# Seven products within seven products: second-layer outputs by two levels of Winograd's scheme, with weight blocks kept in DRAM

## The chip, the cores and the metric

The kernel runs on one core of one Trainium2 chip. The metric is the device time of one execution in microseconds (us). Engines are named as in the profile: PE multiplies matrices, DVE, ACT and POOL (VectorE, ScalarE, GpSimd) work elementwise, SP issues most DMAs. A PE result goes to PSUM, of which there are eight banks of 128 x 512 f32.

## The reference

The reference has two parts. The first is an attention in both directions between tokens x (8 batches, 8 heads, 512 tokens, 64 values) and 32 states per head. Its result, 8 x (512 + 32) rows of 512 values, goes through a feed-forward layer of 2048 hidden units:

```
scores = x @ state^T / 8;  a = softmax(scores);  xread = a @ state
scores2 = state @ x^T / 8; a2 = softmax(scores2); sread = a2 @ x
x2 = concat([xread, sread]) as rows (8 * 544) x 512
h = x2 @ w_in            # 512 x 2048
g = h * cos(h)
out = g @ w_out          # 2048 x 512
```

Everything is f32.

## The kernel before, in words

The main loop (L965) runs over 144 tiles. For each batch b there are 16 tiles; tile f is 128 hidden units for all 512 tokens of the batch, held transposed (hidden unit on the partition, token along the row). Sixteen more tiles take the state rows of all batches at once (256 columns). The attention of batch b+1 is done in parts beside the tiles of batch b, by a plan written out by hand (`plan`, L875: which part at which step on which engine). Attention and `w_in` are merged: `products` (L430) multiplies states with `w_in`, giving `sw`, and the first layer is then `sw` times the softmax weights `aT` (K = 256). Order on every engine is the order of the program text (`manual_schedule`, L56).

A tile goes through `hidden` (L463: two matmuls into a PSUM bank `h`), `gate` (L560, ACT: round to an integer), `gate2` (L564, DVE: difference), `gate3` (L567, ACT: sine) and `gate4` (L571, DVE: times h, into the SBUF array `g_all`).

Both layers use seven block products in place of eight (Winograd's form of Strassen's scheme). In the first layer this is done for tiles of batches 2 to 7 whose `phase` is under 3 (`seven`, L474). Two tiles f, f+1 go together: `hidden_a` (L521) and `hidden_b` (L544) make seven products of 256 columns in PSUM, and `sums_a` (L534) and `sums_b` (L551) add them up on DVE in SBUF (ACT copies one half first, L531). The sums of weight blocks (`sw_sums`, L496) are made on POOL, those of `aT` (`halves`, L482) on DVE.

In the second layer, two batches make a `Pair` (L585). The pair's hidden rows are four blocks (its `phase`: batch even or odd, hidden units lower or upper half), `w_out` is four blocks a11 to a22 with sums s1 to s4 kept in SBUF (`blocks`, L949). Differences of hidden blocks, of 128 x 512 each, are taken one tile at a time by `minus` (L579), on POOL or DVE. Each product is eight tiles times two matmuls of 512 columns (`product`, L617), accumulated in two of four PSUM banks `acc`. A tile's output products (`output`, L698) come `LAG` = 3 tiles after its gates, so the first layer and the gates run ahead of the outputs; p7 and p4 of a pair are done among the tiles of the next pair (`more`, L600). `keep_product` and `plus` (L629, L624) take a product to the array `held`; `store` (L646) transposes it on DVE and sends it by four DMAs on SP. The state rows' outputs are made at the end (`state_products`, L762), again by seven products.

Weights come as f32 bit patterns from DRAM and are converted in steps 0 to 16 (`convert_part`, L215, on ACT, DVE and POOL). A few dummy matmuls (`warm`, L837) fill PE at the start.

The names steps, periods and end are used so: a step is one turn of the main loop; a period is the 32 steps of a pair; the end is steps 128 to 143 (state tiles) and `state_products`.

## Time and profile before

| | us |
|---|---|
| median of 3 runs | 758.56 |
| lowest, highest | 758.52, 759.78 |
| the profiled execution | 759.83 |
| its span, first to last instruction | 758.0 |
| PE busy in the span | 747.9 |
| DVE, ACT, POOL busy | 519.9, 313.2, 256.6 |

A group of the profile gives line, engine, operation and tiles, then the time in which at least one of its instructions ran and the mean of one. Matmuls overlap in a pipeline, so a mean of 599 ns for a matmul pass of 512 columns is not its price; the distance from one to the next is. PEld is the weight load, which runs beside the matmul before. Idle time has behind it what ended it.

### The profile page before, as it was taken

How to read it: one execution, taken by the hardware profiler on the slowest of the kernel's cores; microseconds unless marked ns; L12 is line 12 of the kernel's file. 1: busy time of each engine (PE TensorE's matmuls, PEld its weight loads, DVE VectorE, ACT ScalarE, POOL GpSimd, SP SyncE). 2: the span in 40 equal slices, each digit the busy share in tenths (PEclk: the TensorE clock that was granted, in tenths of full speed). 3: DMA queues.
4: the chain of work that ended last, by engine and by line, in shares of the span. 5: the costliest groups of instructions: out<-in, count | busy, mean ns of one | idle time of the engine just before them, and what ended most of it. 6: DMA issues, size and time to landing. Idle time of an engine off the chain costs nothing.

```text
span 758.0 us, 8557 instructions
## 1 busy us (share of the span) xinstructions
PE 747.9 (99%) x2928; PEld 389.7 (51%) x2928; DVE 519.9 (69%) x883; ACT 313.2 (41%) x522; POOL 256.6 (34%) x265
## 2 busy tenths in 40 slices
PE   8998999999999999999999999999999999999998
PEld 3443443445555554445555554445555554466666
DVE  5778778736886788846886888747877675434630
ACT  3887843533363435333363336432453333212210
POOL 2354278777121212663121113661121126510000
PEclk9999999999999999999999999999999999999999
DMA  8595471060012510160104310350100110101031
GB/s 249 169 277 200 137 105 29 4 108 1 5 23 37 100 23 10 23 117 0 19 11 75 64 29 1 50 90 1 28 1 1 28 29 0 29 0 29 8 48 28
DMA packets 161291, 41.46 MB, mean 55 GB/s; under 512 B 154016, under 2 KB 154528, under 8 KB 161248
## 3 DMA queue, kind: packets, MB, share of 16 engines
q1 hardware_dynamic: 160160, 40.39, 25.3%
q10 hardware_dynamic: 960, 0.39, 0.2%
q8 instruction: 23, 0.38, 0.2%
q14 instruction: 20, 0.16, 0.1%
q0 software_dynamic: 128, 0.13, 0.1%
HBM read 31.98 MB, written 8.91 MB: 54 GB/s over the span
## 4 chain that ended last, share of the span: by engine, by line
PE 92%; DVE 3%; ACT 1%; DMA 1%; POOL 1%; issue 1%; SPq 0%; DVEq 0%; ACTq 0%; POOLq 0%
PE o L619 51%; PE h L466 15%; PE h L509 14%; PE at L314 5%; PE o L772 2%; PE at L404 2%; PE o L314 1%; PE at L772 1%; PE at L387 1%; DMA x_b<-in_x_dram 1%; ACT q L568 0%; DVE i L328 0%; ACT q L562 0%; PE o L840 0%; POOL g_all L581 0%
## 5 line engine op out<-in xcount | busy, mean ns | idle before, releaser
L619 PE MATMUL o<-g_all,w_out 128*128 128x512 f32 x512 | 237.4, 599 | 0.6 <-POOL w_out L237 0.3
L619 PE MATMUL o<-g_all,s 128*128 128x512 f32 x384 | 177.3, 598 | 0.0
L581 POOL TENSOR_TENSOR g_all<-g_all 128x512 f32<-128x512 f32 x89 | 124.7, 1422 | 107.2 <-DVE g_all L575 107.2
L619 PEld LDWEIGHTS o<-g_all,w_out 128*128 128x128 f32 x512 | 93.8, 190 | 108.6 <-issue 102.6
L568 ACT ACTIVATE q<-q,halfpi 128x512 f32<-128x512 f32 (+1 forms) x144 | 100.7, 700 | 91.1 <-DVE q L565 90.9
L619 PEld LDWEIGHTS o<-g_all,s 128*128 128x128 f32 x384 | 70.8, 190 | 88.1 <-issue 84.4
L466 PE MATMUL h<-aT,sw 128*128 128x512 f32 x224 | 106.4, 598 | 2.9 <-DVE g_all L575 2.4
L562 ACT ACTIVATE q<-g_all 128x512 int32<-128x512 f32 x75 | 46.8, 624 | 142.2 <-DVE g_all L555 141.8
L565 DVE TENSOR_TENSOR q<-q,h 128x512 f32<-128x512 int32 (+1 forms) x69 | 42.9, 622 | 81.6 <-ACT q L562 81.5
L562 ACT ACTIVATE q<-h 128x512 int32<-128x512 f32 (+1 forms) x69 | 37.6, 545 | 108.0 <-PE h L466 108.0
L565 DVE TENSOR_TENSOR q<-q,g_all 128x512 f32<-128x512 int32 x75 | 52.9, 705 | 36.0 <-ACT q L562 36.0
L466 PEld LDWEIGHTS h<-aT,sw 128*128 128x128 f32 x224 | 41.9, 190 | 56.6 <-issue 45.7
L504 POOL TENSOR_TENSOR swS<-sw 128x128 f32<-128x128 f32 x35 | 17.6, 502 | 147.6 <-PE h L509 107.3
L575 DVE TENSOR_TENSOR g_all<-g_all,q 128x512 f32<-128x512 f32 x75 | 54.2, 722 | 14.3 <-ACT q L568 14.3
L575 DVE TENSOR_TENSOR g_all<-h,q 128x512 f32<-128x512 f32 (+1 forms) x69 | 42.9, 622 | 22.8 <-ACT q L568 21.9
L504 POOL TENSOR_TENSOR swS<-sw,swS 128x128 f32<-128x128 f32 x35 | 18.3, 523 | 87.1 <-PE h L509 86.7
L509 PEld LDWEIGHTS h<-aT,sw 128*128 128x128 f32 x144 | 27.4, 190 | 34.4 <-issue 28.5
L509 PE MATMUL h<-aS,sw 128*128 128x256 f32 x144 | 43.1, 381 | 0.1
L509 PE MATMUL h<-aT,sw 128*128 128x256 f32 x144 | 42.8, 379 | 0.0
L509 PE MATMUL h<-aS,swS 128*128 128x256 f32 x144 | 42.8, 379 | 0.0
L237 POOL TENSOR_TENSOR w_in<-w_in,s 128x1024 int32<-128x1024 int32 (+1 forms) x10 | 19.3, 1932 | 36.8 <-DVE w_in L232 22.0
L466 PE MATMUL h<-st_all,w_in 128*128 128x256 f32 x128 | 30.2, 379 | 0.0
(109 smaller groups left out, 889.0 us busy)
## 6 DMA issues: line engine op xcount, KB each, us to landing
g_all<-in_moe_w_out_dram SPq DMA_DIRECT2D x8, 1024.0 KB, 5.1
out_dram<-ot SPq DMA_DIRECT2D x128, 64.0 KB, 2.0
g_all<-in_moe_w_in_dram SPq DMA_DIRECT2D x6, 1024.0 KB, 5.3
xT<-in_x_dram SPq DMA_DIRECT2D x96, 64.0 KB, 2.3
x_b<-in_x_dram SPq DMA_DIRECT2D x24, 256.0 KB, 4.6
x_b<-in_x_dram SPq DMA_DIRECT2D x16, 128.0 KB, 4.0
g_all<-in_moe_w_in_dram SPq DMA_DIRECT2D x4, 512.0 KB, 6.0
s<-in_state_dram SPq DMA_DIRECT2D x8, 32.0 KB, 7.3
```

The source lines that it names most:

```text
L237: nc.gpsimd.tensor_tensor(bits, bits, e, op=ALU.add)
L314: nc.tensor.matmul(out=(to or at)[j][Ns * k:Ns * k + Ns, 0:n], lhsT=w[D * j:D * j + D, self.b, Ns * k:Ns * k + Ns], rhs=r(slice(D * j, D * ...
L466: nc.tensor.matmul(out=t.hp, lhsT=t.lhs(i), rhs=t.rhs(i), start=(i == 0), stop=(i == t.kn - 1))
L504: engine.tensor_tensor(o, x1, x2, op=op)
L509: nc.tensor.matmul(out=out, lhsT=w, rhs=r, start=True, stop=True)
L562: nc.scalar.activation(t.q.bitcast(I32), t.hp, func=ACTF.Copy, bias=0.25)
L565: nc.vector.tensor_tensor(t.q, t.q.bitcast(I32), t.hp, op=ALU.subtract)
L568: nc.scalar.activation(t.q, t.q, func=ACTF.Sin, bias=halfpi, scale=-TWO_PI)
L575: nc.vector.tensor_tensor(t.g, t.hp, t.q, op=ALU.mult)
L581: engine.tensor_tensor(out, a, b, op=ALU.subtract)
L619: nc.tensor.matmul(out=acc[bank][ch], lhsT=w[:, i, P * ch:P * ch + P], rhs=g.g, start=(i == 0), stop=(i == NH - 1))
L772: nc.tensor.matmul(out=x, lhsT=b(i), rhs=w[:, i, :], start=(start and i == 0), stop=(i == NH - 1), skip_group_check=True)
```

## The change

The second layer's products are split once more: each of a pair's seven products (eight tiles times 256 output columns) becomes seven products of half the size in every direction. Only p1 and p2 of the first pair stay as they were. In the code:

- `Product` is one of the outer seven; its seven `stage`s are the inner products, each of four matmuls of 256 columns. They share two PSUM banks, b and c: a stage writes half a bank, ACT copies a half into the other bank as a seed (k = 0) or to SBUF (k = 1), later stages add to what is there, and DVE adds two halves (k = 2, 4). `out` then takes a bank to `held` as before, and POOL adds totals.
- `sums` makes the four inner sums of hidden blocks on POOL (128 x 4 x 256 each). The outer differences (`outer_sum`) now go by four tiles at once (128 x 2048), five per pair on DVE and three on POOL.
- `inner_weights` makes the inner sums of the seven outer weight blocks on POOL in steps 9 to 26, and SP writes the 56 blocks of 256 KB to DRAM. `fetch_block` reads one per stage into a ring of four; at the end `load_end_weights` reads those for the state rows. `weight_sum` makes the outer weight sums on DVE.
- `plan_products` sets the stages at a fixed pace: 49 stages over a period of 32 steps, for the last pair 28 stages over 15 steps. There is no `LAG` any more. The products of a pair lie in the period after its own, apart from p1, p2 and p5.
- In the first layer, `seven_part` and `seven_sum` replace `hidden_a`, `hidden_b`, `sums_a` and `sums_b`: the seven products are put together within two banks, in four parts over two steps, two steps ahead of the gates; ACT makes two copies, DVE two additions, and the gates read PSUM. The pool of banks `h` grows from two to four, `acc` shrinks from four to two.
- Loads of x are put in a list and sent by `load_now`, eight per step at first and then four.

The diff, cut to its core:

```diff
-    hps = ctx.enter_context(tc.tile_pool(name="hps", bufs=2, space=PSUM))
+    hps = ctx.enter_context(tc.tile_pool(name="hps", bufs=4, space=PSUM))
...
+    QT, NQUAD = 4, 12
+    g_all = consts.tile([P, (NQUAD + 1) * QT, S], F32)
+    TEMPS = 4
+    quads_free = list(range(TEMPS))
+    def quad(n):
+        return g_all[:, QT * n:QT * n + QT]
+    def matrix(n):
+        return quad(n).rearrange("p t (u d) -> p (t u) d", d=HD)
+    a11, a12, a21, a22 = [matrix(n) for n in range(5, 9)]
+    w_out = ((a11, a12), (a21, a22))
+    NB = 4
+    ring = [g_all[:, QT * NQUAD + i].rearrange("p (i d) -> p i d", d=P)
+            for i in range(NB)]
+    spare = ctx.enter_context(tc.tile_pool(name="spare", bufs=1,
+                                           space=bass.MemoryType.DRAM))
+    blocks_kept = spare.tile([7, 8, P, QT * P], F32)
...
+    aS_all = consts.tile([P, 2, 4, HS], F32)
+    p5_all = consts.tile([P, 2, HS], F32)
+    swS_all = consts.tile([P, 2, 3, P], F32)
...
+    def load_now(n):
+        for _ in range(min(n, len(loads_due))):
+            dst, src = loads_due.pop(0)
+            nc.sync.dma_start(out=dst, in_=src)
...
-    acc = [[ops.tile([P, S], F32, name=f"o{m}{ch}") for ch in range(2)]
-           for m in range(2)]
+    acc = [ops.tile([P, S], F32, name=f"o{ch}") for ch in range(2)]
+    def side_banks():
+        return [hps.tile([P, S], F32, name="h") for _ in range(2)]
...
+    def seven_part(t, k):
+        (b11, b12, b21, b22), swS = weights_of(t)
+        aT, aS = aT_of[t.b], aS_all[:, t.b % 2]
+        if k == 0:
+            t.h1, t.h2 = side_banks()
+        h1, h2 = t.h1, t.h2
+        for out_, w, r, start in (
+                ((h2[:, LO], b11, aT[:, 0, LO], True),
+                 (h2[:, HI], swS[:, 0], aS[:, 0], False)),
+                ((h2[:, LO], swS[:, 1], aS[:, 1], False),
+                 (h1[:, LO], b12, aT[:, 1, LO], False)),
+                ((h2[:, LO], b21, aS[:, 2], False),
+                 (h1[:, HI], swS[:, 2], aT[:, 1, HI], False)),
+                ((h2[:, LO], b22, aS[:, 3], False),))[k]:
+            nc.tensor.matmul(out=out_, lhsT=w, rhs=r, start=start, stop=True,
+                             skip_group_check=True)
+        if k == 0:
+            nc.scalar.copy(h1[:, LO], h2[:, LO])
+            nc.scalar.copy(p5_all[:, 0], h2[:, HI])
+    def seven_sum(t, k):
+        h1, h2 = t.h1, t.h2
+        o = (h1, h2)[k][:, HI]
+        nc.vector.tensor_tensor(o, h2[:, LO], p5_all[:, 0], op=ALU.add)
...
+        row = t.row
+        if t.i % QT == 0:
+            quads_of[row].append(quads_free.pop(0))
+        t.slot = QT * quads_of[row][t.i // QT] + t.i % QT
+        t.g = g_all[:, t.slot, 0:t.n]
...
+    ORDER = (0, 4, 5, 1, 6, 2, 3)
+    WEIGHTS = {"p1": 0, "p2": 1, "p4": 2, "p5": 3, "p6": 4, "p7": 5, "p3": 6}
+    def quarters(m):
+        m = m.rearrange("p (k i) (m d) -> p m k i d", k=2, m=2)
+        return m[:, 0, 0], m[:, 0, 1], m[:, 1, 0], m[:, 1, 1]
+    def inner_weights(which, m, engine=None):
+        m11, m12, m21, m22 = quarters(m)
+        t1, t2, t3, t4 = [quad(TEMPS)[:, n].rearrange("p (i d) -> p i d", d=P)
+                          for n in range(4)]
+        for o, x1, x2, op in ((t1, m21, m22, ALU.add),
+                              (t2, t1, m11, ALU.subtract),
+                              (t3, m11, m21, ALU.subtract),
+                              (t4, m12, t2, ALU.subtract)):
+            (engine or nc.gpsimd).tensor_tensor(o, x1, x2, op=op)
+        for n, block in enumerate((m11, m12, t4, m22, t1, t2, t3, m21)):
+            nc.sync.dma_start(
+                out=blocks_kept[which, n].rearrange("p (i d) -> p i d", d=P),
+                in_=block)
+    stage_list = []
+    def fetch_block(n):
+        if n < len(stage_list):
+            product_, k = stage_list[n]
+            nc.sync.dma_start(
+                out=ring[n % NB].rearrange("p i d -> p (i d)"),
+                in_=blocks_kept[WEIGHTS[product_.name], ORDER[k]])
+    def sub(engine, o, x1, x2):
+        engine.tensor_tensor(o, x1, x2, op=ALU.subtract)
+    class Product:
+        def __init__(self, name, pr, row):
+            self.name, self.pr, self.row = name, pr, (pr.n, row)
+            self.n = len(products)
+            self.b, self.c = acc[1 - self.n % 2], acc[self.n % 2]
+            self.in_place = name in ("p3", "p7", "p4")
+            self.frees = name in ("p3", "p6", "p7", "p4")
+            products.append(self)
+            self.first = len(stage_list)
+            stage_list.extend((self, k) for k in range(len(ORDER)))
+        def quads(self):
+            return [quad(q) for q in quads_of[self.row]]
+        def sums(self, k):
+            lo, hi = self.quads()
+            engine = nc.gpsimd
+            if k == 1:
+                self.q1 = quads_free.pop(0)
+                self.t1 = quad(self.q1)[:, :, LO]
+                self.t2 = quad(self.q1)[:, :, HI]
+                sub(engine, self.t1, lo[:, :, HI], lo[:, :, LO])
+            elif k == 2:
+                sub(engine, self.t2, hi[:, :, HI], self.t1)
+            elif k == 3:
+                self.t3 = lo[:, :, HI]
+                if not self.in_place:
+                    self.q3 = quads_free.pop(0)
+                    self.t3 = quad(self.q3)[:, :, LO]
+                sub(engine, self.t3, hi[:, :, HI], lo[:, :, HI])
+            else:
+                sub(engine, self.t1, hi[:, :, LO], self.t2)
+        def stage(self, k):
+            pr, b, c = self.pr, self.b, self.c
+            lo, hi = self.quads()
+            o, g, start = ((c[:, LO], lo[:, :, LO], True),
+                           (c[:, HI], self.t1, False),
+                           (c[:, LO], self.t2, False),
+                           (b[:, LO], hi[:, :, LO], False),
+                           (c[:, LO], None, False),
+                           (b[:, HI], hi[:, :, HI], False),
+                           (c[:, LO], self.t1, False))[k]
+            if k == 4:
+                g = self.t3
+            for i in range(QT):
+                nc.tensor.matmul(out=o, lhsT=ring[(self.first + k) % NB][:, i],
+                                 rhs=g[:, i], start=(start and i == 0),
+                                 stop=(i == QT - 1), skip_group_check=True)
+            if k == 0:
+                nc.scalar.copy(b[:, LO], c[:, LO])
+            elif k == 1:
+                nc.scalar.copy(p5_all[:, 1], c[:, HI])
+            elif k in (2, 4):
+                o = (b if k == 2 else c)[:, HI]
+                nc.vector.tensor_tensor(o, c[:, LO], p5_all[:, 1], op=ALU.add)
+                if k == 2:
+                    self.sums(4)
+            elif k == 5:
+                self.out(0, b)
+                if self.frees:
+                    quads_free.extend(quads_of[self.row][1:])
+            elif k == 6:
+                self.out(1, c)
+                quads_free.append(self.q1)
+                if not self.in_place:
+                    quads_free.append(self.q3)
+                if self.frees:
+                    quads_free.append(quads_of[self.row][0])
+        def out(self, ch, bank):
+            pr, name = self.pr, self.name
+            if name in ("p1", "p5"):
+                if ch == 0:
+                    setattr(pr, "u" if name == "p1" else "v", Held())
+                o = pr.u if name == "p1" else pr.v
+                nc.scalar.activation(o.t[:, ch], bank, func=ACTF.Copy,
+                                     scale=TWO_PI)
+                return
+            if name in ("p2", "p3") and ch == 0:
+                pr.o = Held()
+            o = pr.o if name in ("p2", "p3") else pr.u
+            plus(o, ch, bank, pr.v if name == "p3" else pr.u)
+            total = {"p6": pr.o, "p7": pr.v}.get(name) if name[1] in "67" else None
+            if total is not None:
+                nc.gpsimd.tensor_tensor(total.t[:, ch], pr.u.t[:, ch],
+                                        total.t[:, ch], op=ALU.add)
+            if ch == 1 and name != "p3":
+                b, half, src = {"p2": (0, 0, pr.o), "p6": (1, 0, pr.o),
+                                "p7": (1, 1, pr.v if name == "p7" else None),
+                                "p4": (0, 1, pr.u)}[name]
+                store(2 * pr.n + b, half, src)
+    products = []
...
+    def plan_products():
+        for m in range(-1, B // 2):
+            if m < 0:
+                names = [("p5", 0)]
+                begin, pace = 1 + 42 * PERIOD / 49, PERIOD / 49
+            else:
+                names = [("p3", 0), ("p6", 0), ("p7", 0), ("p1", 1),
+                         ("p4", 0), ("p2", 1), ("p5", 1)]
+                begin, pace = PERIOD * (m + 1) + 1, PERIOD / 49
+                if m == B // 2 - 1:
+                    names = [n for n in names if not n[1]]
+                    pace = (NF - 1) / (len(names) * STAGES)
+            for j, (name, later_) in enumerate(names):
+                pr = pairs[m + later_ + (m < 0)]
+                pd = Product(name, pr, ROWS[name])
+                start = begin + j * STAGES * pace
+                for k in range(STAGES):
+                    stage_at[int(start + k * pace + 1e-6)].append((pd, k))
+                for k in (1, 2, 3):
+                    sums_at[int(start + 1e-6) - 3 + k].append((pd, k))
+    plan_products()
+    dve, pool = nc.vector, nc.gpsimd
+    for n in range(B // 2):
+        t4_at = (38, 39) if n < B // 2 - 1 else (37, 38)
+        for r, engine, o, x1, x2, half in (
+                (20, dve, 0, 2, 0, 0), (24, dve, 0, 2, 0, 1),
+                (28, pool, 2, 3, 2, 0), (32, dve, 2, 3, 2, 1),
+                (33, dve, 0, 3, 0, 0), (34, dve, 0, 3, 0, 1),
+                (t4_at[0], pool, 1, 1, 0, 0), (t4_at[1], pool, 1, 1, 0, 1)):
+            outer_at[PERIOD * n + r].append((engine, n, o, x1, x2, half))
+    def outer_sum(engine, n, o, x1, x2, half):
+        o, x1, x2 = [quad(quads_of[n, r][half]) for r in (o, x1, x2)]
+        sub(engine, o, x1, x2)
+    def weight_sum(o, x1, x2, op):
+        dve.tensor_tensor(matrix(o), matrix(x1), matrix(x2), op=op)
...
+    for at_, what in (
+            (9, lambda: inner_weights(0, a11)),
+            (13, lambda: inner_weights(1, a12)),
...
            (17, lambda: weight_sum(SQ, A21, A22, add_)),
...
+            (27, lambda: quads_free.extend([A12, SQ, TEMPS]))):
+        weights_at[at_].append(what)
+    n_stages = 0
+    def stages(step, n=100):
+        nonlocal n_stages
+        for pd, k in stage_at[step][0:n]:
+            pd.stage(k)
+            n_stages += 1
+            fetch_block(n_stages + NB - 2)
+        del stage_at[step][0:n]
+    def plain(u):
+        return u.b >= 2 and not seven(u)
...
+        near = all_tiles[step + 1:step + 2] + all_tiles[step + 2:step + 3]
+        even = step % 2 == 0
+        coming = None
+        if even and len(near) > 1 and seven(near[1]):
+            coming = near[1]
+        if not even and near and seven(near[0]):
+            coming = near[0]
+        if step >= NF:
+            gate(t) if t.b >= 2 else None
+        if coming:
+            seven_part(coming, 0 if even else 2)
+            if even:
+                coming.hp, all_tiles[step + 3].hp = coming.h1, coming.h2
+        if t.b < 2 and step != 1:
             hidden(t)
-        first = len(ahead) > 1 and seven(ahead[0]) and ahead[0].f % 2 == 0
-        if first:
-            if not seven(t):
-                h = t.hp
-                take_slot(t)
-                nc.scalar.copy(t.g, h)
-            hidden_a(*ahead)
+        if near and plain(near[0]):
+            hidden(near[0])
...
+            if t.b < 2:
                 gate(t)
             gate2(t)
+            if coming and not even:
+                seven_sum(coming, 1)
             if step == 3:
-                warm(4, acc[MAIN][0])
+                warm(4, acc[0])
                 part(0, "products", 1, SIDE)
-            if first:
-                sums_a(ahead[0])
+            stages(step, 1)
...
+        if coming:
+            seven_part(coming, 1 if even else 3)
+            if even:
+                seven_sum(coming, 0)
...
+        for what in weights_at[step]:
+            what()
+        for what in outer_at[step]:
+            outer_sum(*what)
+        for pd, k in sums_at[step]:
+            pd.sums(k)
+        if t.b < B - 1 and t.b > 0 and s in (11, 12):
+            halves(t.b + 1, s - 11)
+        if 4 <= step < 4 + NH:
+            first_product(pairs[0], step - 4)
+        if 12 <= step < 12 + 2 * NH and even:
+            second_product(pairs[0], (step - 12) // 2)
+        if step == 24:
+            for n in range(NB - 1):
+                fetch_block(n)
+        stages(step)
+        load_now(H if step < NF else 4)
+        if step == PERIOD * (B // 2) - 8:
+            load_end_weights(2)
+        if t.pair is None and t.n_th > 3 and len(quads_free) > 2:
+            load_end_weights(1)
```

## The prediction

> **What bounds the kernel now.** I read the page first (busy shares, slices, chain), then a table of windows cut at steps 0, 16, 28, 32, 64, 96 and 128 of the main loop (the starts of `gate2`, L565, give these times), then single groups, then the timeline. On the page look at PE: busy in every slice at full clock, and 92% of the chain that ended last.
>
> ```profile
> span 758.0 us, 8557 instructions
> PE 747.9 (99%) x2928; PEld 389.7 (51%) x2928; DVE 519.9 (69%) x883; ACT 313.2 (41%) x522; POOL 256.6 (34%) x265
> PEclk9999999999999999999999999999999999999999
> PE 92%; DVE 3%; ACT 1%; DMA 1%; POOL 1%; issue 1%; SPq 0%; DVEq 0%; ACTq 0%; POOLq 0%
> L531 ACT COPY g_all<-h 128x256 f32<-128x256 f32 x36 | 13.3, 371 | 32.5 <-PE h L509 32.5
> ```
>
> The windows (columns: length, then busy time of PE, PEld, DVE, ACT, POOL) show where other engines are near it: in steps 0 to 15 ACT is busy 64.1 of 75.8 us, and in steps 16 to 27 DVE and POOL 40 to 42 of 52.1. From step 28 on PE alone sets the pace.
>
> ```profile
> 24.70:100.50 75.80, 73.11 (x340) 31.80 (x339) 59.67 (x88) 64.08 (x87) 30.43 (x15) 0.98 0.68 192
> 100.50:152.60 52.10, 52.10 (x194) 22.43 (x195) 40.33 (x59) 22.86 (x36) 42.43 (x27) 1.00 0.20 36
> 152.60:177.40 24.80, 24.65 (x92) 11.18 (x91) 10.00 (x23) 7.49 (x14) 17.07 (x14) 1.00 0.47 82
> 343.20:509.00 165.80, 165.80 (x667) 86.02 (x666) 125.75 (x213) 67.00 (x117) 51.81 (x68) 1.00 0.23 39
> 666.50:758.00 91.50, 87.58 (x319) 60.15 (x317) 34.42 (x87) 14.67 (x33) 0.35 (x1) 0.99 0.13 23
> ```
>
> The price of a matmul is its issue distance, not its mean duration. Each f32 matmul is two passes; weight loads of 512-column passes stand 0.43 us apart, and those of 256 columns 0.22 (403.59, 403.81). So 512 columns cost 0.853 us and 256 columns 0.427: the smaller shape costs nothing extra.
>
> ```profile
> 401.45 0.19 PEld L619 LDWEIGHTS o<-g_all,w_out 128*128 128x128 f32 x1 [0.24 <-issue]
> 401.88 0.19 PEld L619 LDWEIGHTS o<-g_all,w_out 128*128 128x128 f32 x1 [0.24 <-issue]
> 403.59 0.19 PEld L509 LDWEIGHTS h<-aT,sw 128*128 128x128 f32 x1 [0.24 <-issue]
> 403.81 0.19 PEld L509 LDWEIGHTS h<-aT,swS 128*128 128x128 f32 x1
> ```
>
> Last, DVE and POOL get in each other's way. A multiply with two SBUF inputs usually takes 0.69 us; here it takes 1.88, and ends just after POOL's pair (180.83 + 4.67 = 185.50). The third line gives min/median/max of a 1024-element one.
>
> ```profile
> 180.83 4.67 POOL L950 TENSOR_TENSOR w_out<-w_out 128x1024 f32<-128x1024 f32 x2
> 184.17 1.88 DVE L575 TENSOR_TENSOR g_all<-g_all,q 128x512 f32<-128x512 f32 x1
> L381 DVE TENSOR_TENSOR aT<-aT,xT x8: 1208/1232/2075, 19.9 to 557.5; 128x1024 f32<-128x1024 f32 x8
> ```
>
> **What the Trainium skill says.** "SBUF — State Buffer", section "Who interferes with whom": a DVE instruction with two SBUF inputs contends with a GpSimd instruction that reads SBUF, and the later one blocks; with at most one SBUF input it doesn't (outside certain modes). The 1.88 us agrees. "PSUM — Partial Sum Buffer", section "PSUM bank collisions raise a hardware error": two engines may not be in one bank at once, even at different columns, so they have to be ordered by bank. No run shows a collision, but the built order of the new kernel waits by bank: a stage that writes one half waits for the copy out of the other half. Same page, "The four PSUM rules": only matmuls set the written bits, and a matmul without start adds where they are set; so a copied seed can be added to. No row of before shows it.
>
> **The change, part by part.** Counts are from the two built programs, durations from the rows of before.
>
> 1 PE. Removed: 448 output matmuls of 512 columns. Added: 32 of 512 and 728 of 256. (448 - 32) x 0.853 - 728 x 0.427 = -44.4 us. The first layer's counts do not change. By step, at these prices, PE's work changes so: steps 0-15, 68.7 to 65.3; 16-27, 50.4 to 36.8; 28-31, 24.3 to 22.1; each period of 32 steps, 161.1 to 149.2 (the last 154.3 to 142.8); the end (steps 128-143 and state products) 88.7 to 99.0. So 19 us are taken out of the start and 10 are put into the end, since the last pair's four remaining products lie among the state tiles.
>
> 2 Start. Steps 16-27 get four weight sums and two outer differences of 2048 elements on DVE. L381's 1.23 us for 1024, with 1.05 ns per further element (from 0.69 at 512), gives 2.31 each: low end 2.31, high end 2.31 plus a POOL operation of 2.34 (L950); I take 2.31 + 0.6. DVE's own sum becomes 51 us, with these waits 54.5, plus some 4 for the spots where nothing fills the 0.72 us between `gate2` and `gate4`: 58 against 52.1, +6. POOL's 28 quarter sums (28 x 1.28 = 36 us, partly in place of 19 us of `blocks`) and 56 writes of 256 KB lie beside it; SP's queue waits there for POOL's t4, and the token loads behind have four steps of slack; I take 0, and up to 8 us if DVE must wait for these writes before it overwrites a sum. Steps 0-15: ACT-bound, -1; steps 28-31: -1. Start: +4.
>
> 3 Gates read PSUM, and 5 sums per two tiles become 2 plus one more copy. DVE saves 15 us per period (132 to 118); it was hidden, so it's worth 0 by itself.
>
> 4 POOL. Per period 28 sums of 4x256 (2.34 each), 3 outer ones (4.67), 4 totals (1.28), 12 sets of weight sums (4 x 0.46): 107 us of 165, from 52. Not the bound by sum, but the weight sums (`sw_sums`) now stand behind long operations and are due one step later.
>
> 5 The new waits. Before, an LAG of three tiles stood between first layer and outputs. Now PE holds, in one order, parts of the first layer that wait for ACT or DVE within the same step; behind each waits everything on PE. By hand through one period:
> (a) Outer differences at steps 64-66. After the stage's end: ACT's copy 0.60, two `products_kept` 1.17, `gate3` 0.72, DVE `gate4` 0.68, outer 2.31, next `gate2` 0.68, `seven_sum` 0.41 = 6.6 us. PE has two pairs of parts and a stage, 0.85 + 0.85 + 1.71 = 3.4. It waits 3.2, and again some 2.3 after step 66, where no `products_kept` lie in the chain but DVE is already late: 5.5. Low end 0 (DVE ahead by then), high end one POOL operation more for each, 10. The one at step 52: 1.5.
> (b) `exps` (1.28 table load, 1.06, two of 0.88) ahead of the seed copy on ACT: 2.3 once a period.
> (c) `total` on POOL waits for DVE's `plus`, and `sw_sums` stands behind it: 0.68 + 1.28 + 0.46 + hops 0.2 = 2.6 after the stage, PE has 0.85: 1.7, twice (low 0, high 4 if an outer sum of 4.67 is in POOL's way too).
> (d) Stages next to each other on PE in tiles without the seven products: stage k=3 waits for `plus`-like DVE work on the same bank (0.41 + 0.2): 1 us per period.
> Sum 13.7 per period against 12.0, 12.0 and 11.5 saved: +6 for three periods; I take off 3 for small waits of before that go with the replaced parts (its period took 165.8 for 161.1 of work). +3.
>
> 6 End. +10.3, and 12 dependent stage pairs, half of them adjacent, 0.6 each: +14.
>
> 7 Queues. Token and x loads, sent before in one go (16 tokens took SP 13.7 us), are sent four per step, so that block reads and stores are not behind all of them: 0, since a batch's loads still have ten steps. End weights: 28 reads among the state tiles, the last due after step 142; at most one landing of 4.6 us late, 0 taken. Block reads: 182 of 256 KB on SP, asked for three stages ahead (some 9 us). x_b's 256 KB took 4.6 us and 1024 KB took 5.1; at 54 GB/s now there is room. Hidden: 0; if stores that wait on DVE hold SP's queue longer than 9 us, 2 to 4 us each time. Seed copies: PSUM to PSUM isn't in the trace; 0.37 (L531) low, 0.6 high; 0.37 taken.
>
> Sum: 4 + 3 + 14 = +21 on the span of 758.0; that run took 759.83, 1.3 above the median of 758.56, so the median becomes 758.6 + 21 = 779.
>
> **Rivals.** First, PE stays fed: waits (a) to (d) vanish in run-ahead. Then only the start's gain is lost (DVE's sum there stands) and 35.5 - 10.3 - 4 - 4 = 17 us are gained: 742; if the start gains too, 722. For it: PE's chain share and POOL's 194 us of waiting for PE (slack). Against: steps get 4.3 us of PE work, less than the chain gate to gate4 plus an outer sum. This ends on the other side; it decides if waits per period stay under 6 us. Second, the shared port: per period DVE's two-SBUF work (some 19 operations, 13 us of outer and norm) meets POOL busy two thirds of the time; half an operation's wait (1.2 x 0.67) each is 15 us on DVE, and POOL waits as long; half of both reaching PE adds 17 per period: 779 + 51 = 830.
>
> **How the numbers follow.** Forecast (765 to 800) 0.52; PE fed 0.25; port 0.20; within 0.2% 0.03. About 0.2% is what a measurement of this kernel can tell from none. Faster 0.27, same 0.03, slower 0.70. The range reaches from 738 (below the first rival's 742) to 815 (part of the second; its upper half, and a start that gains too, are left out). Most chance is slower; that side alone is 765 to 815.
>
> **What would show it.** Right: PE's share under 93% with idle in steps 64-67, named DVE `seven_sum` and POOL `swS`; steps 16-27 near 58 us; periods near 166; the end near 105. Wrong: periods near 152 (waits hidden), DVE outer differences above 4 us or POOL's quarter sums above 3 (port), or PE waiting for block reads.

## The result

| median, us | before | after |
|---|---|---|
| timed together, 4 runs of each | 759.17 (758.52 to 760.58) | 845.37 (843.84 to 847.43) |
| ratio, 95% interval | | 1.113 [1.110, 1.117] |
| span of the profiled execution | 758.0 | 845.5 |

The change makes the kernel 86 us slower. The forecast had the sign, with +21 us, and the time lies outside its range. The page of the kernel as changed, in the lines that answer to those of before (busy times, granted clock, chain):

```profile
PE 746.9 (88%) x3552; PEld 520.8 (62%) x3552; DVE 531.2 (63%) x787; ACT 332.6 (39%) x612; POOL 491.4 (58%) x332
PEclk9999997799999999899999998999999999999999
PE 51%; DVE 15%; issue 3%; ACT 2%; POOL 2%; DMA 2%; SPq 1%; DVEq 0%; ACTq 0%; POOLq 0%
```

PE has 44 us less work by count, yet is busy as long as before (746.9 against 747.9), and idle for 99 us where it was idle for 10. Its clock dips in slices where it was 9 throughout. Its share of the chain fell from 92% to 51%, and DVE's rose from 3% to 15%.

The windows of after, cut at the same steps (0, 16, 28, 32, 64, 96, 128). Columns: length, busy time of PE, PEld, DVE, ACT, POOL, then granted clock, DMA share, GB/s.

```profile
25.10:106.70 81.60, 73.63 (x335) 31.57 (x333) 63.12 (x88) 64.62 (x88) 41.84 (x23) 0.98 0.70 216
106.70:172.20 65.50, 49.58 (x168) 21.46 (x168) 53.02 (x61) 21.94 (x36) 42.32 (x25) 0.82 0.72 207
172.20:193.60 21.40, 18.49 (x91) 12.52 (x99) 12.48 (x21) 7.79 (x16) 17.54 (x13) 1.00 0.75 152
193.60:378.50 184.90, 163.63 (x842) 120.87 (x834) 118.79 (x177) 72.72 (x143) 111.72 (x83) 0.96 0.44 104
378.50:563.20 184.70, 164.53 (x842) 121.26 (x834) 117.44 (x177) 72.86 (x144) 111.80 (x84) 0.96 0.46 105
563.20:734.10 170.90, 154.52 (x757) 117.18 (x742) 97.97 (x150) 65.08 (x128) 109.98 (x76) 0.97 0.42 107
734.10:845.50 111.40, 101.19 (x460) 86.32 (x458) 53.30 (x94) 16.62 (x42) 49.73 (x21) 1.00 0.45 128
```

Beside the same cuts of before (columns in us; the start counts from 0 to step 32, the periods are steps 32 to 127):

| | before | after | difference | forecast |
|---|---|---|---|---|
| start | 177.4 | 193.6 | +16.2 | +4 |
| of it steps 16 to 27 | 52.1 | 65.5 | +13.4 | +6 |
| three periods | 489.1 | 540.5 | +51.4 | +3 |
| end | 91.5 | 111.4 | +19.9 | +14 |

The prediction shows the second period of before, and the first is like it in length and in PE's busy time. The third:

```profile
509.00:666.50 157.50, 157.50 (x573) 82.48 (x572) 107.57 (x182) 58.95 (x102) 49.66 (x63) 1.00 0.09 14
```

PE was busy through all 489.1 us of the three periods. Now it is busy for 482.7 of 540.5 us and idle for 57.8. So the 51.4 us more are 57.8 us of waits less 6.4 us of busy time, where PE's counts alone promised 35.5 us less. No other engine is full in a period: DVE is busy 117 of 185 us and POOL 112.

The second period shows which waits. PE is idle there for 184.7 - 164.5 = 20.2 us. Three groups in that window name 19.6 of it: after the last bar stands the idle time just before the group's matmuls, and what ended it.

```profile
L726 PE MATMUL o<-g_all 128*128 128x256 f32 x392 | 98.5, 397 | 5.9 <-issue 2.7 <-DVE o L735 2.4 <-DMA g_all<-blocks_kept 0.5
L537 PE MATMUL h<-aS_all,swS_all 128*128 128x256 f32 x48 | 15.0, 395 | 7.2 <-POOL swS_all L518 4.3 <-ACT p_all L541 2.9
L537 PE MATMUL h<-aS_all,sw 128*128 128x256 f32 x48 | 14.9, 392 | 6.5 <-DVE h L546 6.5
```

13.7 of the 20.2 us stand before the first layer's parts (`seven_part`, L537): for the addition on DVE, the weight sums on POOL and the copy on ACT, which the forecast had named. The other excess is inside PE's busy time: 164.5 us for what costs 149.2 by the prices of the forecast.

One place shows both, in the timeline (start, duration, instruction, wait):

```profile
418.53 6.82 POOL L674 TENSOR_TENSOR g_all<-g_all 128x2048 f32<-128x2048 f32 x2
419.90 3.17 DVE L360 TENSOR_SCALAR m<-m 128x2 f32<-128x2 f32 x1
420.93 1.89 PE L726 MATMUL o<-g_all 128*128 128x256 f32 x8
424.93 0.39 ACT L540 COPY h<-h 128x256 f32<-128x256 f32 x1
425.77 1.10 PE L537 MATMUL h<-aS_all,swS_all 128*128 128x256 f32 x2 [2.95 <-ACT p_all L541]
427.51 2.77 PE L726 MATMUL o<-g_all 128*128 128x256 f32 x8
```

POOL takes a difference of 2048 elements (the first of the two) at 418.53. DVE's scaling of two numbers per partition, 0.17 us at its shortest, takes 3.17 beside it, and the exponentials of L374 on ACT wait for that number. The two copies (L540 and L541) are behind them on ACT, the next parts behind the copies on PE, which stands still for 2.95 us. After that eight passes take 2.77 us in place of 1.89, since the clock has dropped. Windows over the same place (clock is the third number from the end):

```profile
422.80:425.80 3.00, 0.05 (x2) 0.06 (x1) 1.59 (x4) 2.67 (x8) 2.55 (x2) 1.00 0.27 87
425.90:429.30 3.40, 3.40 (x9) 2.69 (x10) 3.33 (x8) 2.23 (x3) 0.00 (x0) 0.50 0.00 0
429.30:433.30 4.00, 4.00 (x31) 2.55 (x30) 2.33 (x4) 0.99 (x3) 1.28 (x1) 1.00 0.23 66
```

The Trainium skill, "TensorE: Matmul & The Clock Gate", section "Part 1: The HAM clock gate (the "warmup" mystery)", states that PE's clock falls to half after an idle window of some 3.4 us and comes back after some 3.4 us of work. The spell of 3.4 us at 0.50 agrees; the idle time just ahead of it, 2.95 us, was shorter than the page's window. Before, no slice of the page showed a lower clock, and the forecast had no such term.

### The profile page after: what moved, and what is told of

It is laid out like the page before. It is cut to its first block, busy times and chain, and to the rows that moved or that the text cites. A ratio compares the mean times of both kernels' runs of the same rounds, so it can differ in the third digit from the quotient of the medians.

```text
span 845.5 us, 10499 instructions
## 1 busy us (share of the span) xinstructions
PE 746.9 (88%) x3552; PEld 520.8 (62%) x3552; DVE 531.2 (63%) x787; ACT 332.6 (39%) x612; POOL 491.4 (58%) x332
## 4 chain that ended last, share of the span: by engine, by line
PE 51%; DVE 15%; issue 3%; ACT 2%; POOL 2%; DMA 2%; SPq 1%; DVEq 0%; ACTq 0%; POOLq 0%
PE o L726 29%; PE h L537 10%; PE h L485 5%; DVE g_all L674 4%; PE at L328 2%; PE at L821 2%; POOL held L765 2%; DVE q L557 1%; DMA g_all<-blocks_kept 1%; DVE g_all L569 1%; DVE g_all L793 1%; DVE m L360 1%; DVE h L546 1%; DVE held L592 1%; PE at L418 1%
## 5 line engine op out<-in xcount | busy, mean ns | idle before, releaser
L674 POOL TENSOR_TENSOR g_all<-g_all 128x1024 f32<-128x1024 f32 (+1 forms) x116 | 309.6, 2682 | 143.8 <-PE o L726 67.5
L726 PE MATMUL o<-g_all 128*128 128x256 f32 x1456 | 361.8, 395 | 21.4 <-DVE o L735 10.6
L726 PEld LDWEIGHTS o<-g_all 128*128 128x128 f32 x1456 | 279.8, 196 | 101.6 <-issue 40.6
L557 DVE TENSOR_TENSOR q<-q,h 128x512 f32<-128x512 int32 (+1 forms) x144 | 93.5, 649 | 61.1 <-ACT q L554 61.0
L569 DVE TENSOR_TENSOR g_all<-h,q 128x512 f32<-128x512 f32 (+1 forms) x144 | 93.4, 649 | 46.6 <-ACT q L560 46.0
L554 ACT ACTIVATE q<-h 128x512 int32<-128x512 f32 (+1 forms) x144 | 81.7, 568 | 15.6 <-PE h L485 15.6
L537 PE MATMUL h<-aS_all,swS_all 128*128 128x256 f32 x144 | 45.2, 396 | 21.6 <-POOL swS_all L518 12.8
L537 PE MATMUL h<-aS_all,sw 128*128 128x256 f32 x144 | 44.9, 394 | 21.1 <-DVE h L546 20.5
L592 DVE SCALAR_TENSOR_TENSOR held<-o,held 128x512 f32<-128x512 f32 x40 | 27.5, 689 | 56.7 <-PE o L726 56.6
L735 DVE TENSOR_TENSOR o<-o,p_all 128x256 f32<-128x256 f32 x52 | 22.3, 429 | 64.2 <-PE o L726 64.1
L657 POOL TENSOR_TENSOR g_all<-g_all 128x512 f32<-128x512 f32 x28 | 44.6, 1611 | 21.3 <-DMA blocks_kept<-g_all 11.9
L674 DVE TENSOR_TENSOR g_all<-g_all 128x2048 f32<-128x2048 f32 x20 | 54.0, 2702 | 0.0
L537 PEld LDWEIGHTS h<-aS_all,sw 128*128 128x128 f32 x144 | 25.6, 189 | 32.3 <-DVE h L546 16.6
L537 PEld LDWEIGHTS h<-aS_all,swS_all 128*128 128x128 f32 x144 | 27.2, 195 | 28.8 <-POOL swS_all L518 15.5
L537 PE MATMUL h<-aT,sw 128*128 128x256 f32 x144 | 44.7, 394 | 0.0
L256 POOL TENSOR_TENSOR w_in<-w_in,aS_all 128x1024 int32<-128x1024 int32 (+1 forms) x10 | 19.3, 1928 | 36.8 <-DVE w_in L251 23.8
```

Of the source, the lines that this page charges most:

```text
L537: nc.tensor.matmul(out=out_, lhsT=w, rhs=r, start=start, stop=True, skip_group_check=True)
L554: nc.scalar.activation(t.q.bitcast(I32), t.hp, func=ACTF.Copy, bias=0.25)
L557: nc.vector.tensor_tensor(t.q, t.q.bitcast(I32), t.hp, op=ALU.subtract)
L569: nc.vector.tensor_tensor(t.g, t.hp, t.q, op=ALU.mult)
L592: nc.vector.scalar_tensor_tensor(out=out.t[:, ch], in0=bank, scalar=TWO_PI, in1=b.t[:, ch], op0=ALU.mult, op1=ALU.add)
L657: (engine or nc.gpsimd).tensor_tensor(o, x1, x2, op=op)
```

## The experiments

The theory tested here: the excess is made of separate waits in PE's one order (the first layer's parts, the outer differences ahead of the gates, the totals, adjacent stages), and each costs more than its length, since the clock falls behind it. Rivals: the port between DVE and POOL stretches both engines; the block traffic delays PE; in the end, waits by bank. Changes below are of medians against after's 845.37. The kernel before, timed anew beside each set of runs, had medians of 759.2 to 760.4. The kernel as changed was not timed again, so a difference of 1 to 2 us can't be told from none. Stages come from one profiled execution, which isn't always a typical one, and a single stage moves by up to some 3 us between kernels that don't touch it.

**First layer as eight products.** The differences of `aT` stay.

```diff
     def seven(t):
-        return t.pair is not None and t.b > 1 and t.phase < 3
+        return False
```

> The first layer's seven products are switched off everywhere (each tile is made by two plain matmuls, one step ahead), all else is the changed kernel. PE gets more work: per pair of tiles 3.41 instead of 2.99 us, 36 pairs, +15.4 us. Waits theory (PE stands in steps 32 to 127 because first-layer parts wait for a copy, an addition or a weight sum of the same step): 845 + 15 - 3 x 20 = 800. Port theory (DVE and POOL hold each other up): weight sums of 66 us leave POOL, so about 835. DMA theory (block reads and writes late): 860.

815.51: -29.9 us. The periods take 174.3, 174.4 and 160.3, 10 to 11 us less each, though PE has 24 tiles x 0.213 = 5.1 us more work in each. So some 16 us of each period went with the parts: by the profiles 10.6 us of idle time and, for the work done, 5 of busy time. The total lies between the 800 of the waits theory and the 835 of the port. It bounds the price of the parts' waits: the parts went together with their weight sums on POOL, additions on DVE and copies on ACT.

**No block reads after the first four.** The stages use whatever block lies in the ring.

```diff
     def fetch_block(n):
-        if n < len(stage_list):
+        if n < NB:
```

> Left out: all block reads after the first four, so the stages use weight blocks that are not theirs. Waits theory: block reads are hidden, 840 to 845. DMA theory: the reads share engines with x loads and stores and come late, 815 or less.

841.48 (838.4 to 844.6), -3.9, with periods at 179.6, 182.8 and 169.0. DRAM reads are not where the time is.

**No inner sums on POOL.** The stages take blocks of the hidden rows in place of `sums`.

```diff
-                sub(engine, self.t1, lo[:, :, HI], lo[:, :, LO])
-            elif k == 2:
-                sub(engine, self.t2, hi[:, :, HI], self.t1)
+                self.t1, self.t2 = lo[:, :, HI], hi[:, :, HI]
...
-                sub(engine, self.t3, hi[:, :, HI], lo[:, :, HI])
-            else:
-                sub(engine, self.t1, hi[:, :, LO], self.t2)
```

> Left out: the four inner sums of hidden blocks per product on POOL (104 operations, 246 us of POOL); stages read unsummed blocks. Port theory: POOL is then busy a quarter of the time, DVE's two-input operations run free, 800. Waits theory: only the lateness of weight sums and totals on POOL goes, about 5 us per period, 825 to 835.

825.51, -19.9: POOL is busy 232 us in place of 491, and the periods are 6 to 9 us shorter. This bounds what the port and POOL's queue together can have cost through these sums; the theory of the port alone had 800.

**No outer differences.** `outer_sum` does nothing; the products use rows without them.

```diff
-        o, x1, x2 = [quad(quads_of[n, r][half]) for r in (o, x1, x2)]
-        sub(engine, o, x1, x2)
+        return
```

> Left out: the outer differences of hidden blocks (20 of 128x2048 on DVE, 12 on POOL). Waits theory: on DVE each stands in front of the next gate and addition that PE waits for; five per pair at about 2 us each with the slow clock after it, -30 to -40, so 805 to 815. Port theory: 56 us leave POOL and 54 leave DVE, most of it beside PE, 825.

808.26, -37.1; the periods take 171.9, 170.6 and 159.7. It takes away DVE's and POOL's work and the waits at once, so it only bounds them.

**Plain tiles' matmuls on both sides of a stage.** For tiles without the seven products, one of the two matmuls of `hidden` goes behind the first stage of the step, so that two stages are not adjacent there.

```diff
         if near and plain(near[0]):
-            hidden(near[0])
+            hidden(near[0], 0)
...
+        if near and plain(near[0]):
+            hidden(near[0], 1)
         stages(step)
```

> The same work; in tiles without the seven products (second half of odd batches, and the state tiles at the end) a tile's first-layer matmuls are issued in two halves, one ahead of the step's first stage, one between it and the last stage, so that two stages seldom stand next to each other on PE. Bank theory (a stage waits for the copy or addition out of the same bank that the stage before it set off, 0.6 us and more): the end of 111 us falls by 5 or more, periods by 3 each, 830. If DVE or POOL are late there in any case: 840 to 846.

835.47, -9.9: 12 us out of the three periods by the profiles, and only 1.5 out of the end, where 5 or more were expected. But 10 of the 12 us are PE's busy time, since the clock was higher (0.97 to 0.99), and the waits of stages in the plain tiles are still there. From this kernel's list for its second period (L728 and L737 are L726 and L735 of the kernel as changed):

```profile
PE o L728 <- issue: 3.1, 1, 3.1
PE o L728 <- DVE o L737: 2.4, 1, 2.4
```

The timeline of the kernel as changed shows where the same two waits come from:

```profile
513.09 0.38 ACT L730 COPY o<-o 128x256 f32<-128x256 f32 x1
513.57 2.74 PE L726 MATMUL o<-g_all 128*128 128x256 f32 x8 [2.20 <-issue]
520.55 2.74 DVE L674 TENSOR_TENSOR g_all<-g_all 128x2048 f32<-128x2048 f32 x1
524.28 1.98 PE L726 MATMUL o<-g_all 128*128 128x256 f32 x5 [2.40 <-DVE o L735]
```

The first ends with ACT's copy, which stands behind exponentials as at 419 (ACT is busy with them from 509.5 to 513.1). The second waits for an addition behind an outer difference on DVE. So adjacency isn't their cause, and the gain of this run, most of it clock, doesn't price it.

**Totals on DVE.**

```diff
-                nc.gpsimd.tensor_tensor(total.t[:, ch], pr.u.t[:, ch],
+                nc.vector.tensor_tensor(total.t[:, ch], pr.u.t[:, ch],
```

> The same work; the 16 totals go from POOL to DVE, so that no weight sum stands behind an operation on POOL that waits for DVE. Waits theory, step (c) of the prediction: 1.7 us twice a period and a slow clock after it, 845 - 3 x 4 = 833, less some 0.7 us per total that DVE now does: 835. Port theory: DVE gets more two-input work, 848.

836.10, -9.3, as expected. POOL's weight sums no longer stand behind a total that waits for `plus`: PE's 4.3 us of waits for them in the second period are gone from its list, and part of them came back at other places (idle 19.3 in place of 20.2 us in that period, 7.6 less in all three).

**Three of seven weight sets made and written.** The products of the last four use the blocks of p1, p2 and p4.

```diff
-    WEIGHTS = {"p1": 0, "p2": 1, "p4": 2, "p5": 3, "p6": 4, "p7": 5, "p3": 6}
+    WEIGHTS = {"p1": 0, "p2": 1, "p4": 2, "p5": 0, "p6": 1, "p7": 2, "p3": 0}
...
     def inner_weights(which, m, engine=None):
+        if which > 2:
+            return
```

> Left out: the quarter sums and DRAM writes of four of the seven outer weight blocks (16 sums on POOL and 32 writes in steps 19 to 26); their products use the blocks of the others. The outer weight sums on DVE stay. Write theory (DVE stands in steps 22 and 25 until the writes of the old sum are out of its memory): steps 16 to 27 fall from 65.5 to 56, all in all 835. If DVE's own work is the bound there: 842 to 846.

839.08, -6.3, and steps 16 to 27 take 58.6 in place of 65.5. Half of a cause: it takes away POOL's sums, the writes and the waits for them at once.

**Outer differences behind the gates.** Those on DVE go behind the step's gates and one is moved to POOL.

```diff
-                (20, dve, 0, 2, 0, 0), (24, dve, 0, 2, 0, 1),
-                (28, pool, 2, 3, 2, 0), (32, dve, 2, 3, 2, 1),
-                (33, dve, 0, 3, 0, 0), (34, dve, 0, 3, 0, 1),
+                (21, dve, 0, 2, 0, 0), (25, dve, 0, 2, 0, 1),
+                (28, pool, 2, 3, 2, 0), (32, pool, 2, 3, 2, 1),
+                (33, dve, 0, 3, 0, 0), (35, dve, 0, 3, 0, 1),
...
             if coming and not even:
                 seven_sum(coming, 1)
+            for what in outer_at[step]:
+                if what[0] is dve:
+                    outer_sum(*what)
```

> The same work; each outer difference on DVE is put behind the addition that PE waits for in an odd step (steps 21, 25, 33 and 35 of a period), not at the end of the step before, and the fifth (step 32) goes to POOL. Waits theory: of the 13 us a period that fell away without the outer differences, 8 to 10 fall away here, 815 to 822. Port theory: the same two-input work on DVE, more on POOL, 845 or more.

826.85, -18.5, half of what leaving the differences out gives, with all of the work still done. It misses the 815 to 822 of the waits theory, but is far from the 845 or more of the port. In the second period the waits for DVE ahead of the parts fall from 6.5 to 2.7 us. So the place in DVE's order counts; what part of it is the one difference that went to POOL, this run doesn't tell.

**Those three edits together** (plain tiles, totals, outer differences).

> The plain tiles' matmuls put between two stages, the totals moved to DVE, and the outer differences put behind the gates: alone they gave -10, -9 and -19 us. Theory of separate waits in PE's one order: the gains add up, 845 - 38 = 807, periods near 170. Rival, one resource (the port, or DVE's queue) behind all three: they overlap, and the best alone stays the measure, 822 to 827. The end stays at 111 and steps 0 to 27 at 147 in both.

807.65, -37.7; the single gains were 9.9 + 9.3 + 18.5 = 37.7. They add up, as separate waits would, and a common resource behind them (822 to 827) would not. That they do so to the last digit is chance: the four runs lie between 802.4 and 808.1. The profiled one is the fastest of them, while that of the kernel as changed was the slowest of its four. Its second period (columns as above) shows what the clock can cost:

```profile
364.10:535.20 171.10, 156.98 (x842) 116.98 (x834) 120.85 (x180) 73.09 (x143) 109.11 (x81) 1.00 0.49 114
```

In the second period the same 842 matmul records take PE 157.0 us at a clock of 1.00, against 164.5 at 0.96. Of the 13.6 us that this period gains, 7.5 are PE's busy time (4% of 185 is 7.4) and 6.1 are idle time. Its clock was 1.00 in all three periods, and PE's busy time there is 463.1 us in all, 19.6 less than the 482.7 of the kernel as changed. Since the longest of four executions is compared with the shortest of four, a typical pair may differ by less.

Nor is the clock simply the price of each idle spell. PE still stands still for some 3 us at three places in this period, and the clock stays up behind all of them. One of them, the same wait for the copies as at 422.8 above:

```profile
404.10:407.00 2.90, 0.00 (x0) 0.02 (x1) 1.49 (x4) 2.63 (x8) 2.50 (x2) 1.00 0.27 90
407.00:410.40 3.40, 3.39 (x16) 2.85 (x16) 3.33 (x9) 2.37 (x3) 0.00 (x0) 1.00 0.00 0
```

In the first period of the kernel without block reads, too, PE was idle for 22.1 us at a clock of 1.00. What decides whether the clock falls behind a spell of 2 to 3 us, no run here shows.

**More matmuls in steps 16 to 27.** There the clock was lowest, 0.82. The first layer's matmuls are issued twice.

```diff
-        for i in range(t.kn):
+        for i in list(range(t.kn)) * (2 if t.b == 1 and t.f < 12 else 1):
```

> The first layer's matmuls of steps 16 to 27 are issued twice, 24 more of 512 columns, 20 us of PE at full clock, with the same result. Theory of the clock: PE idles less, its clock stays up, and the stage keeps its 65.5 us or falls to about 60 in spite of 20 us more work, with a granted clock above 0.95. Rival, the clock only follows idle that others set, and matmuls stand on the path: the stage grows by a good part of the 20 us, to 75 or more, total 855 to 865. The other stages don't change.

845.79, +0.4 us, for 20 us more of PE's work. The window has a clock of 0.97 and a length of 66.8:

```profile
106.20:173.00 66.80, 60.57 (x212) 27.29 (x212) 52.96 (x60) 22.66 (x36) 42.90 (x25) 0.97 0.72 202
```

Here PE is off the path, and the low clock only follows its idle time. What sets these steps is DVE: 53.0 busy, and its waits in the kernel as changed, from the list of waits (total, times, longest):

```profile
DVE g_all L1047 <- DMA blocks_kept<-g_all: 7.6, 2, 4.8
DVE q L557 <- ACT q L554: 2.6, 1, 2.6
DVE g_all L569 <- ACT q L560: 2.1, 5, 0.8
```

53.0 + 7.6 + 2.6 + 2.1 = 65.3 of 65.5 us. 7.6 are for DRAM writes of weight blocks that must have ended before DVE overwrites the sum that they read.

**The same writes from another source.** The last four sets are written from `a12`, so nothing waits for them to end; POOL's sums and all bytes stay.

```diff
+        kept = (m11, m12, t4, m22, t1, t2, t3, m21)
+        if which > 2:
+            kept = quarters(a12) * 2
-        for n, block in enumerate((m11, m12, t4, m22, t1, t2, t3, m21)):
+        for n, block in enumerate(kept):
```

> The four last sets of weight blocks (p5, p6, p7, p3) are written to DRAM from a12, which nothing overwrites in these steps, in place of the sums; as many bytes, the same queues, and POOL still makes the quarter sums, but the sums that wait in the kernel as changed for such a write to end don't any more. What leaves the kernel for these four products is made with a12's blocks. Theory of the writes (7.6 us of DVE's waits and 11.9 of POOL's): steps 16 to 27 fall from 65.5 to about 58, which is DVE's own sum with its gate waits; the total to about 838. Rival, the queue of SP or POOL's pace holds the stage: it stays above 63.

837.61, -7.8; steps 16 to 27 take 56.7, and the waits for `blocks_kept` are gone from DVE's list.

```profile
104.80:161.50 56.70, 46.37 (x168) 19.24 (x168) 51.83 (x59) 22.04 (x37) 40.05 (x25) 0.88 0.93 247
```

51.8 us of these are DVE's work, and 4.7 the two gate waits that stayed. The cost of the waits for the writes is shown by this; it is as large as what the three-set kernel gained.

**State tiles' inner sums on POOL.** In the end DVE's sums of 128 elements (L793) meet POOL's long ones: four of them take 5.21 us (1.03 for four of them where POOL is not in the way), and the addition that PE's next stage waits for is behind them.

The edit, in `state_sums`:

```diff
-            nc.vector.tensor_tensor(o, x1, x2, op=ALU.subtract)
+            nc.gpsimd.tensor_tensor(o, x1, x2, op=ALU.subtract)
```

> The state tiles' four inner sums go from DVE to POOL. Theory of the port (in the end DVE's two-SBUF sums of 128 elements stand behind POOL's long sums, and gate2 and the stage's addition stand behind them): the end falls from 111 to about 104, total 838. Rival, dependent stages on PE set the end: it stays within 2 us of 111. Second rival, POOL's own queue becomes the wait: the end grows to 115. The periods stay at 185, 185, 171.

844.67, -0.7, which is nothing that can be told from none; yet the end takes 107.3 in place of 111.4 (PE's waits there for the addition on DVE fall from 3.5 to 1.1), and the second period 187.8. Undecided by itself; it is taken up in the last kernel.

**Differences of `aT` on POOL.** The DVE operations that were stretched most beside POOL (L504, 0.42 to 4.62 us) go to POOL.

```diff
-            nc.vector.tensor_tensor(aS[:, i], x1, x2, op=ALU.subtract)
+            nc.gpsimd.tensor_tensor(aS[:, i], x1, x2, op=ALU.subtract)
```

> The differences of aT's quarters go from DVE to POOL, four for each batch. On DVE they took 9.4 us in the second period, 8 of them, for 3.4 at their shortest. Theory of the port: DVE is rid of 9.4 us per period in one place, where PE waits for it, and the periods fall by 3 to 6 us each, total 830 to 836. Rival, the separate waits alone: PE isn't waiting there, or waits for POOL in its place; periods within 2 us of 185, 185, 171, total 842 to 850.

849.13, +3.8. The periods take 183.1, 184.8 and 170.5: nothing moved, though 9.4 us of DVE's time left the second. PE's list of waits in that period begins so:

```profile
PE h L537 <- DVE h L546: 6.5, 7, 2.0
PE h L537 <- POOL swS_all L518: 4.3, 2, 2.6
```

These are the sums of the kernel as changed, and the next two, 2.9 and 2.7, are too. So in the periods these stretched operations were off PE's path. In the start, steps 16 to 27, which DVE sets, got 4.1 us shorter, but steps 28 to 31 grew from 21.4 to 30.6: PE now waits there 5.0 us in one go for POOL's weight sums.

**Three edits, and eight products in the first layer.**

> The three edits together with the first layer as eight products in place of seven (alone -30 us). If all four waits are separate: 845 - 68 = 777, periods near 159 (their PE work is then 154). If the first layer's parts and the three edits repair the same waits: 795 to 805, periods near 168. Below the 759 of the kernel before it can come only if the start and the end (each some 17 to 20 us longer than there) fall too, which no edit here touches.

786.30, -59.1, of 67.6 if all were additive: between the 777 of separate waits and the 795 to 805 of common ones. The repairs overlap by 8 us. That fits the profiles: two of the three edits act on waits ahead of the parts, and without parts these waits are gone already.

**The same, with the state sums on POOL.**

> The three edits, the first layer as eight products, and the state tiles' inner sums on POOL. By the profile the last edit took 4 us out of the end (775 to 817) while the total didn't move. If these 4 us are real: 786 - 4 = 782, the end 105. If they are given back elsewhere: 786, the end 109. The rest over the kernel before (759) lies then in the start, 13 us, and in the end's added matmuls, 10 us.

779.22, -7.1 on the kernel without the last edit, with the end at 102.8 in place of 109.0.

```profile
674.10:776.90 102.80, 99.22 (x460) 86.96 (x458) 36.34 (x65) 17.24 (x42) 60.18 (x50) 0.99 0.49 138
```

Of these, PE is idle for 3.6 us (102.8 - 99.2), where it was for 8.1 without the last edit (109.0 - 100.9). The place that went is this one (start, duration, instruction; L795 and L676 are L793 and L674 of the kernel as changed):

```profile
724.23 9.61 POOL L676 TENSOR_TENSOR g_all<-g_all 128x1024 f32<-128x1024 f32 x4 [4.65 <-PE o L728]
725.39 6.24 DVE L795 TENSOR_TENSOR g_all<-g_all 128x128 f32<-128x128 f32 x4
732.03 1.22 PE L728 MATMUL o<-g_all 128*128 128x256 f32 x2 [4.49 <-DVE o L737]
```

Four short sums on DVE, 1.02 us in all where they run free, take 6.24 beside POOL's, and PE waits 4.49 us for the addition behind them. Without that wait, and the slower clock behind it, the end is 6.2 us shorter. So here the port did hold up PE. This is the fastest version that was tried, and it is still slower than the kernel before, by 1.026 [1.024, 1.028]. By its stages it is 12.7 us longer in the start, 5.1 shorter in the periods and 11.3 longer in the end.

## Why the forecast was right in sign and wrong in size

**Step 1, PE's counts: right.** 1456 passes of 256 columns stand on the page (728 products of two passes), and eight weight loads of L726 in 1.7 us keep the 0.21 to 0.22 us at full clock. What failed is the next thing: that PE would work these off at the old pace.

**Step 2, the start (+4 forecast, +16.2 measured).** The failing sentence is "I take 0, and up to 8 us if DVE must wait for these writes". The wait is there with 7.6 us, and taking it away gives 7.8 us back. The rest of the sum for steps 16 to 27 was close: 58 us forecast for DVE with its gate waits, 57.7 without the writes (53.0 + 2.6 + 2.1). Steps 0 to 15 took 5.8 us more, not 1 less. PE is idle there for 8.0 us in place of 2.7; its list of waits has two new ones, 2.3 us for ACT's copy to `held` (L588) and 1.7 us for loads of x. No run takes them away, so this cause stays open.

**Steps 3, 4 and 7: mostly right.** DVE's busy time fell (118 in a period) with no gain; POOL's sum of 107 us per period was 112; block reads are hidden but for at most 4 us of the whole. The seed copy took 0.37, the low bound (366 ns in the mean of 36 on the page's line L540).

**Step 5, the waits (+3 forecast, +51.4 measured): here it failed.** The sum was 13.7 us of waits a period less 1 of old ones, against 12 saved. Over the three periods:

| us | forecast | measured |
|---|---|---|
| waits of PE | +38.1 | +57.8 |
| PE's busy time | -35.5 | -6.4 |

The larger failure is in the second row, in the term "12.0, 12.0 and 11.5 saved". It takes the price of a matmul at full clock and puts a slower clock at nothing, without a reason. The clock was 0.96 to 0.97 in these periods. At 1.00, in the kernel with the three edits, PE's busy time was 26.0 us below before; so up to 19.6 of the missing 29.1 us are the clock. The other 9.5 us are there at full clock too: PE was busy 4.7 us a period longer than the sum of prices before, and 7.8 now. What these are, no run shows.

The first row has the right mechanism and too small a size. The waits of PE in the second period, by the forecast's own places:

- (a) Outer differences: 7.0 forecast with the one at step 52. At these places 3.8 were measured, and all of it went when the differences were put behind the gates. The one four steps later, at step 56 of the first period, wasn't in the sum; in the second it is the 2.4 us shown with the plain tiles (3.7 us when moved behind the gates).
- (b) Behind `exps`: 2.3 forecast, once a period. A period has two batches, and PE waited twice, 2.95 and 2.2 us. In the first of these DVE's scaling, stretched beside POOL, holds up the exponentials by 1.65. No run took (b) alone.
- (c) Weight sums behind the totals: 3.4 forecast, 4.3 measured (2.6 and 1.7). They went with the totals.
- (d) Adjacent stages: 1 forecast. No wait over 0.7 us is left for them.
- Seven waits of 0.5 to 0.7 us, 4.3 together, four of them for the addition ahead of the parts, weren't in the sum.

So 15.6 of the 20.2 us are at the kinds of places that the forecast named, and little is in ordinary tiles. The 3 us taken off for old waits weren't there: PE of before had no idle time in its periods, and the excess of its busy time over the prices grew.

**Step 6, the end (+14 forecast, +19.9 measured).** The difference leaves 9.6 us for more than the added work, not 3.6. Taking the state sums off DVE gives 4.1 us in the kernel as changed and 6.2 in the last kernel, so the port, which the step had not counted, is a good part of it.

**The rivals.** "PE stays fed" is refuted by PE's idle time. "Shared port" gave 830, nearer to the result, yet for a reason that the runs bear out only in part. DVE operations were stretched, by 6.0 us in a period for L504 and 3.0 for L360, but moving L504 away changed no period. The signs set for it, DVE's outer differences above 4 us and POOL's quarter sums above 3, show in single ones (4.05 and 3.33 at the longest), not in the medians (2.46 and 1.27). The port is on the path in single places (L360, L793), not in proportion to the overlap. The sum that led to 830 is also wrong: half of 15 us on DVE and 15 on POOL is 15 a period, not 17. Of the forecast's own signs PE's share (88%) and the waits for `seven_sum` and POOL's sums came; the lengths of 58, 166 and 105 us did not (65.5, 185 and 111).

## What to carry to other kernels

When an order with slack (here three tiles between producer and consumer on PE) is replaced by one in which a result goes out to another engine and back within a step, find every place where something long stands in that way and cost each of them, in all batches: here 15.6 of 20.2 us of idle time in a period were at eight such places, and two of them were overlooked. Fewer matmuls on a full engine are worth their count only while it stays fed: the idle time is paid, and the clock may fall as well. That second price was up to 19.6 us here beside 57.8 of idle time, and it didn't come behind every idle spell, so carry it as a range. Look into the profile of an experiment too: the one with the plain tiles was faster, but not at the waits that it was made for. A sum that a DMA still reads is a buffer in use, so overwriting it waits for the write's end.

## What the runs showed of the hardware

- Half clock after idle: a spell of 3.4 us at 0.50 behind 2.95 us of idle in the kernel as changed, none behind 2.90 us of idle at the same place in the kernel with three edits. The difference over a period was up to 4% (164.5 against 157.0 us for the same 842 matmul records). In steps 16 to 27, where PE was off the path, a clock of 0.82 cost nothing, and 24 more matmuls raised it to 0.97 for no time.
- A DVE operation on two numbers per partition took 3.17 us beside a POOL subtraction, 0.17 at its shortest. It has one SBUF input. The Trainium skill, "SBUF — State Buffer", section "Who interferes with whom", counts `tensor_scalar` among the operations that can take the port shared with GpSimd; this agrees, and the forecast had looked only at operations with two inputs.
- Four DVE sums of 128 elements took 6.24 us beside POOL's sums and 1.02 without them; the longest single one took 2.43 us, about as long as a POOL sum of 1024 elements (2.36): a short operation can wait for most of a long one.
